# Changing the start of an attention and gated-MLP kernel: dummies, transpose order, one load's queue, and where one column block is accumulated

## The chip, the cores and the metric

The kernel runs on one core of a Trainium2 chip. The metric is the device time of one execution in microseconds. Where "slow execution" is said below, a difference of one or two us is meant. Most numbers of this document come from the profile of one execution per kernel. Its span (first to last instruction) is some 2 us shorter than the device time of the same execution.

## The reference, cut to what matters

```python
def reference(A_x, A_k_cache, A_v_cache, A_wq, A_wo, B_x, B_W_gate, B_W_up, B_W_down):
    xn = _layernorm(A_x)                     # A_x: 1 x 2048 x 512, bf16
    s = _A_ref(xn, A_k_cache, ...)           # attention, 32 heads of 128, 2048 keys, then @ wo
    gate = xn @ B_W_gate                     # 512 -> 1792
    up = xn @ B_W_up
    h = relu(gate) * up
    g = silu(h @ B_W_down)
    return A_x + s * g
```

The part at stake is the very start: load the first 512 rows of x, normalise, transpose, and begin the gate and up products of those rows.

## The kernel before: the parts that matter

TensorE (PE) needs the rows transposed. For the first 512 rows, the kernel only centres them on VectorE (DVE), transposes on PE into the two accumulator banks `ps_acc`, and copies to `xcT` on ScalarE (ACT). Four "tiles" of 128 rows are handled one by one, so that PE can begin early. The scale is put in later.

The first three column blocks of 128 columns ("head blocks" 0 to 2) are computed tile by tile, with 128-column matmuls. They hold the three double-bank slots of a ring in `ps_r`. Column block 3 and later ones use 512-column matmuls over all four tiles.

```python
warm_w = sem_ln1.sig(dve.memset(warm[:], 0.0))
load_x0(sp, 0)                        # 128 rows each
load_x0(act, 1)
load_w(sp, Wg_sb, wg_src, sem_wg, 0)  # gate columns 0..383
load_w(act, Wu_sb, wu_src, sem_wu, 0) # up columns 0..383
load_x0(sp, 2)
load_x0(act, 3)
...
def head_ln():
    ctok = {0: head_transpose(0, head_center(0))}
    warm_mm(2)
    for n in range(4):
        if n + 1 < 4:
            ntok = head_center(n + 1)
        _wait(pe, ctok[n])            # ScalarE's copy of tile n
        head_tile(n, 0)               # 4 gate + 4 up matmuls of 128 columns
        if n + 1 < 4:
            ctok[n + 1] = head_transpose(n + 1, ntok)
        for fc in range(1, HFC):      # HFC = 3
            head_tile(n, fc)
...
# emit_gate_up, for fc >= HFC:
s = ring_acquire()                    # waits until slot s has been read out
...
_wait(pe, warm_w)
warm_mm(10)                           # dummies: 128x512 matmuls on zeros
head_ln()
```

The dummies do no work. They keep PE busy while the first rows are on their way. The Trainium skill (the notes on the chip; "TensorE: Matmul & The Clock Gate", Part 1) says that the array starts at half its clock and is let up after a busy window of about 3.4 us; the windows run freely, whenever the kernel starts. Traces agree about the two rates: dummies start 427 ns apart at first and 216 ns apart later.

The softmax here doesn't subtract the row's maximum and nothing guards it: scores larger than these inputs give would overflow.

## Time and profile before

| | before |
|---|---|
| device time, median (range) of 5 executions | 1286.96 us (1286.37 to 1287.04) |
| span of the profiled execution | 1284.64 us |
| PE busy | 1278.8 us |
| first gate/up matmul | 6.214 us |
| column block 3 starts | 12.834 us |
| span minus start of block 3 | 1271.80 us |

The page's first part, of the kernel before, gives busy time, share of the span, and number of instructions by engine; its chain of waits gives shares of the span:

```profile
PE 1278.8 (100%) x12040; PEld 835.2 (65%) x12040; DVE 380.6 (30%) x685; ACT 1001.7 (78%) x1109; POOL 13.2 (1%) x25
...
PE 99%; DVE 1%; ACT 0%; issue 0%; DVEq 0%
```

PE is never long without work. Only holes in PE's stream, or PE at half clock, can be won back. The holes before 15 us stand in the timeline of that window. Columns: start and length in us, engine, line, operation, output<-inputs, shapes, count; in brackets the idle time before it and what ended it. Only lines that the argument uses are shown.

```profile
1.19 4.12 PE L374 MATMUL ps_r<-warm 128*128 128x512 bf16 x10 [1.19 <-DVE warm L239]
...
5.15 0.39 PE L364 MATMUL ps_acc<-ident,xc_sb 128*128 128x128 bf16 x4
...
5.57 0.58 ACT L369 COPY xcT<-ps_acc 128x512 bf16<-128x512 bf16 x1 [1.79 <-PE ps_acc L364]
5.63 0.35 DVE L354 TENSOR_SCALAR xc_sb<-x_sb,mv 128x512 bf16<-128x512 bf16 x1
6.21 0.40 PE L402 MATMUL ps_r<-xcT,Wg_sb 128*128 128x128 bf16 x4 [0.25 <-ACT xcT L369]
...
8.23 0.39 PE L364 MATMUL ps_acc<-ident,xc_sb 128*128 128x128 bf16 x4
...
8.66 0.59 ACT L369 COPY xcT<-ps_acc 128x512 bf16<-128x512 bf16 x1 [0.98 <-PE ps_acc L364]
...
9.35 0.39 PE L402 MATMUL ps_r<-xcT,Wg_sb 128*128 128x128 bf16 x4
...
11.34 1.57 ACT L454 ACTIVATE gr_sb<-ps_r 128x512 bf16<-128x512 f32 x3 [0.53 <-PE ps_r L402]
...
12.04 0.69 DVE L460 TENSOR_TENSOR hT<-gr_sb,ps_r 128x512 bf16<-128x512 bf16 x1 [2.93 <-PE ps_r L402]
...
12.83 1.02 PE L488 MATMUL ps_r<-xcT,Wg_sb 128*128 128x512 bf16 x4 [0.42 <-ACT gr_sb L454]
```

How to read it: a group of four 128-column matmuls shows 0.39 us, but the next group starts 0.22 us later. One matmul is recorded with 219 ns, of which only the first 56 ns keep the next one from starting. So a hole is measured from start to start, minus 56 ns (216 ns for 512 columns); the bracket shows less.

From 6.21 to 12.25 there is no hole at all. The transposes of tile 2 stand at 8.23, the copy runs 8.66 to 9.25, and tile 2 begins in its turn. Then comes the one hole of 0.58 us, from 12.25 to 12.83: column block 3 needs slot 0, which VectorE finishes reading at 12.73. The bracket blames ScalarE's relu, but the instruction that ended last before PE went on is the VectorE product at 12.04 to 12.73.

### The profile page before, as it was taken

The page shows a single profiled execution, that of the slowest core. Times are in us where ns is not written, and L with a number is a line of the kernel's source. Part 1 is how long each engine was busy: PE and PEld are TensorE (multiplying, and loading weights), DVE is VectorE, ACT ScalarE, POOL GpSimd, SP SyncE. Part 2 cuts the span into 40 slices and gives each one's busy share as a digit, 9 for nine tenths or more (in the row PEclk, how much of TensorE's full clock was granted, in tenths as well). Part 3 has the DMA queues.
Part 4 walks back from the last instruction along what each step waited for, and adds up shares of the span by engine and source line. Part 5 has one row for each costly group of instructions (what it writes and reads, how often), then busy time and mean ns, then how long its engine had stood idle before and what let it go on. Part 6 is the DMA issues. An engine that isn't in the chain of part 4 may idle for free.

```text
span 1284.6 us, 26946 instructions
## 1 busy us (share of the span) xinstructions
PE 1278.8 (100%) x12040; PEld 835.2 (65%) x12040; DVE 380.6 (30%) x685; ACT 1001.7 (78%) x1109; POOL 13.2 (1%) x25
## 2 busy tenths in 40 slices
PE   9999999999999999999999999999999999999998
PEld 5444476666666666666666666666666666666665
DVE  6433311112222222222222222222222222234455
ACT  3322399998888888888888888888888888888884
POOL 2100000000000000000000000000000000000000
PEclk9999999999999999999999999999999999999999
DMA  9600123232222332332321322323323312333202
GB/s 262 131 1 1 22 48 53 62 55 38 36 53 46 71 55 50 55 70 51 54 47 31 66 47 53 55 67 55 55 51 71 54 34 38 51 67 55 51 13 75
DMA packets 240977, 72.13 MB, mean 56 GB/s; under 512 B 227808, under 2 KB 240864, under 8 KB 240864
## 3 DMA queue, kind: packets, MB, share of 16 engines
q1 hardware_dynamic: 240048, 69.76, 28.5%
q8 instruction: 96, 1.57, 0.5%
q10 hardware_dynamic: 816, 0.66, 0.2%
q14 instruction: 17, 0.14, 0.0%
HBM read 32.77 MB, written 2.10 MB: 27 GB/s over the span
## 4 chain that ended last, share of the span: by engine, by line
PE 99%; DVE 1%; ACT 0%; issue 0%; DVEq 0%
PE ps_acc L742 36%; PE ps_r L645 34%; PE ps_r L578 9%; PE ps_r L599 8%; PE ps_acc L511 4%; PE ps_r L488 4%; PE ps_r L492 4%; PE ps_r L779 1%; DVE fin_tmp L787 0%; PE ps_r L402 0%; PE ps_r L374 0%; DVE x_sb L803 0%; ACT gr_sb L454 0%; PE ps_acc L364 0%; ACT xcT L369 0%
## 5 line engine op out<-in xcount | busy, mean ns | idle before, releaser
L655 ACT ACTIVATE PT<-ps_r 128x1024 bf16<-128x1024 f32 x1024 | 952.5, 1054 | 167.7 <-PE ps_r L645 167.7
L742 PEld LDWEIGHTS ps_acc<-V_sb,PT 128*128 128x128 bf16 x8192 | 620.9, 98 | 241.8 <-ACT PT L655 3.5
L742 PE MATMUL ps_acc<-V_sb,PT 128*128 128x129 bf16 x8192 | 776.9, 220 | 0.0
L645 PE MATMUL ps_r<-QT_sb,KT_sb 128*128 128x512 bf16 x2048 | 754.5, 379 | 0.0
L672 DVE RECIPROCAL rz_sb<-ps_acc 128x4 f32<-128x4 f32 x127 | 23.2, 183 | 729.8 <-PE ps_acc L742 729.8
L645 PEld LDWEIGHTS ps_r<-QT_sb,KT_sb 128*128 128x128 bf16 x2048 | 194.9, 98 | 1.1 <-DVE QT_sb L589 0.4
L578 PE MATMUL ps_r<-xnT,Wq_sb 128*128 128x512 bf16 x512 | 130.9, 379 | 0.0
L599 PE MATMUL ps_r<-Wo_sb,OT_store 128*128 128x512 bf16 x448 | 114.6, 379 | 0.0
L589 DVE CAST QT_sb<-ps_r 128x512 bf16<-128x512 f32 x128 | 88.5, 691 | 48.2 <-PE ps_r L578 48.2
L578 PEld LDWEIGHTS ps_r<-xnT,Wq_sb 128*128 128x128 bf16 x512 | 49.8, 97 | 60.7 <-ACT PT L655 27.1
L675 DVE TENSOR_TENSOR Onorm<-ps_acc,rz_sb 128x512 bf16<-128x512 f32 x127 | 87.8, 691 | 4.4
L599 PEld LDWEIGHTS ps_r<-Wo_sb,OT_store 128*128 128x128 bf16 x448 | 43.8, 98 | 52.9 <-ACT PT L655 0.2
L454 ACT ACTIVATE gr_sb<-ps_r 128x512 bf16<-128x512 f32 x56 | 32.9, 595 | 49.2 <-PE ps_r L488 48.7
L612 DVE TENSOR_TENSOR s_acc<-s_acc,ps_r 128x512 f32<-128x512 f32 x96 | 66.0, 687 | 17.4 <-PE ps_r L599 17.4
L460 DVE TENSOR_TENSOR hT<-gr_sb,ps_r 128x512 bf16<-128x512 bf16 x56 | 38.4, 685 | 46.9 <-PE ps_r L492 42.2
L511 PE MATMUL ps_acc<-Wd_sb,hT 128*128 128x512 bf16 x224 | 49.0, 379 | 0.0
L492 PE MATMUL ps_r<-xnT,Wu_sb 128*128 128x512 bf16 x168 | 43.1, 379 | 0.0
L488 PE MATMUL ps_r<-xnT,Wg_sb 128*128 128x512 bf16 x168 | 43.1, 379 | 0.0
L511 PEld LDWEIGHTS ps_acc<-Wd_sb,hT 128*128 128x128 bf16 x224 | 21.9, 98 | 26.5 <-DVE g_sb L528 0.3
L519 ACT ACTIVATE sig_sb<-ps_acc 128x512 f32<-128x512 f32 x12 | 7.2, 597 | 29.5 <-PE ps_acc L511 29.5
L492 PEld LDWEIGHTS ps_r<-xnT,Wu_sb 128*128 128x128 bf16 x168 | 16.4, 98 | 19.8
L488 PEld LDWEIGHTS ps_r<-xnT,Wg_sb 128*128 128x128 bf16 x168 | 16.4, 98 | 19.8
(50 smaller groups left out, 182.1 us busy)
## 6 DMA issues: line engine op xcount, KB each, us to landing
V_sb<-in_A_v_cache_dram SPq DMA_DIRECT2D x32, 512.0 KB, 4.6
Wq_sb<-in_A_wq_dram SPq DMA_DIRECT2D x32, 128.0 KB, 2.5
Wo_sb<-in_A_wo_dram SPq DMA_DIRECT2D x8, 512.0 KB, 4.9
OT_store<-Onorm SPq DMA_TRANSPOSE x127, 2.4
Wd_sb<-in_B_W_down_dram SPq DMA_DIRECT2D x1, 1792.0 KB, 14.6
x_sb<-in_A_x_dram SPq DMA_DIRECT2D x3, 512.0 KB, 12.1
out_dram<-x_sb SPq DMA_DIRECT2D x6, 256.0 KB, 2.2
Wg_sb<-in_B_W_gate_dram SPq DMA_DIRECT2D x1, 768.0 KB, 12.0
```

What stands on the lines that cost most here:

```text
L460: dve.tensor_tensor(hT[par][:, fc, :], gr_sb[gk][:], ps_r[:, gb + 1, :], ALU.mult)
L488: ins = pe.matmul(ps_r[:, gb, :], Wg_sb[:, c, fs], xT[:, c, xs], start=(c == 0), stop=(c == DC - 1))
L492: ins = pe.matmul(ps_r[:, gb + 1, :], Wu_sb[:, c, fs], xT[:, c, xs], start=(c == 0), stop=(c == DC - 1))
L511: ins = pe.matmul(ps_acc[:, jb, 0:D], hT[par][:, fc, j * 128:(j + 1) * 128], Wd_sb[:, fc, :], start=(fc == 0), stop=(fc == FC - 1))
L578: ins = pe.matmul(ps_r[:, bank, :], Wq_sb[b][:, c, :], xnT[:, c, qs], start=(c == 0), stop=(c == DC - 1))
L589: etok = sem_qpe.sig(dve.tensor_copy(QT_sb[b][:, qs], ps_r[:, bank, :]))
L599: ins = pe.matmul(ps_r[:, bank, 0:D], OT_store[g % 2][:, hh, n * 128:(n + 1) * 128], Wo_sb[g % 2][:, hh, :], start=(hh == 0), stop=(hh == ...
L612: dve.tensor_tensor(s_acc[:, n, :], s_acc[:, n, :], ps_r[:, bank, 0:D], ALU.add)
L645: ins = pe.matmul(ps_r[:, 2 * s + tt, :], KT_sb[h % 2][:, t * 128:(t + 1) * 128], QT_sb[h % 2][:, qs], start=True, stop=True)
L655: act.activation(PT[pb][:], ps_r[:, 2 * s:2 * s + 2, :], ACTF.Exp, scale=scale)
L675: dve.tensor_tensor(Onorm[ob][:], o_ap, rz_sb[:].to_broadcast([128, 4, Dh]), ALU.mult))
L742: ins = pe.matmul(o_ap, PT[pb][:, tt, j * 128:(j + 1) * 128], V_sb[vb][:, t, 0:VW], start=(t == 0 and j % 2 == 0), stop=(t == KT - 1 and j ...
```

## The change

Its intent, as its description has it: start the dummies sooner, from constants that exist already, and use fewer of them; put the second tile's transposes ahead of the first gate/up; load rows 256 to 511 through one queue; compute column block 3 in the accumulators, which are idle then, so that it need not wait for a slot.

```diff
-        warm = S_([128, D], BF16, "warm")
...
-                warm_w = sem_ln1.sig(dve.memset(warm[:], 0.0))
                 load_x0(sp, 0)
                 load_x0(act, 1)
                 load_w(sp, Wg_sb, wg_src, sem_wg, 0)
                 load_w(act, Wu_sb, wu_src, sem_wu, 0)
                 load_x0(sp, 2)
-                load_x0(act, 3)
+                load_x0(sp, 3)
...
+                ones_w = nc.const_aps.tensor(1.0, [128, 128], BF16)
+                ones_r = nc.const_aps.tensor(1.0, [128, NQ], BF16)
...
                 def head_ln():
-                    ctok = {0: head_transpose(0, head_center(0))}
-                    warm_mm(2)
+                    ctok = [head_transpose(0, head_center(0))]
+                    warm_mm(1)
+                    ctok.append(head_transpose(1, head_center(1)))
+                    ntok = {2: head_center(2), 3: head_center(3)}
                     for n in range(4):
-                        if n + 1 < 4:
-                            ntok = head_center(n + 1)
                         _wait(pe, ctok[n])
-                        head_tile(n, 0)
-                        if n + 1 < 4:
-                            ctok[n + 1] = head_transpose(n + 1, ntok)
-                        for fc in range(1, HFC):
+                        for fc in range(HFC):
                             head_tile(n, fc)
+                            if fc == 1 and n in (1, 2):
+                                ctok.append(head_transpose(n + 1, ntok[n + 1]))
...
+                def gu_banks(s):
+                    if s is None:
+                        return ps_acc[:, 0, :], ps_acc[:, 1, :]
+                    return ps_r[:, 2 * s, :], ps_r[:, 2 * s + 1, :]
...
-                        s = ring_acquire()
-                        gb = 2 * s
+                        if Q == 0 and fc == HFC:
+                            s = None
+                            _wait_all(pe, acc_free)
+                        else:
+                            s = ring_acquire()
+                        g_ps, u_ps = gu_banks(s)
...
-                _wait(pe, warm_w)
-                warm_mm(10)
+                warm_mm(8)
                 head_ln()
```

The transposes of tiles 2 and 3 stood behind head block 0 of the tile before; now they stand behind head block 1.

## The prediction

> **What bounds the kernel now.** TensorE: the page gives PE 1278.8 of 1284.6 us busy, and the chain of waits is 99% PE. The change touches only the first 15 us, so only PE idle or cold time there can be won. The timeline of that window shows:
>
> - 1.19 us: first dummy, after the VectorE memset of their operand (0.86 to 1.13). Dummies start every 427 ns until 4.58, then every 216 ns; the granted clock record begins at 4.85.
> - The four transposes of tile 0 wait for centred rows (VectorE ends 4.77), then stand behind the tenth dummy: 5.15. ScalarE's copy runs 5.57 to 6.16, the first gate/up starts 6.21.
> - From 6.21 to 12.25 PE streams without a hole: 24 groups of four 128-column matmuls and three groups of transposes, 0.223 us each. Tiles 1 to 3 begin just after their copies end (7.68, 9.25, 10.81): transposes, then two head blocks (0.89 us), nearly exactly cover the 0.39 us to the last transpose's end plus the 0.585 us copy.
> - 12.25 to 12.83: PE waits for ring slot 0 (relu 0 at 11.34, product 0 to 12.73), 0.58 us. After it, PE has no hole.
>
> **What the change does.**
>
> 1. Column block 3 in the accumulators: it need not wait for slot 0. Gain up to 0.58 us.
> 2. Tile 1's transposes before the first gate/up: one group of 0.223 us leaves the stream. But they need VectorE's second centring, which ends 5.98 whatever else moves. So transposes at about 6.08, first gate/up at about 6.30: 0.09 us later, though tile 0's copy is ready some 0.25 us sooner. Net gain 0.13.
> 3. Transposes of tiles 2 and 3 move from after head block 0 to after head block 1. Now only one head block (0.446 us) stands between them and the tile that needs the copy. From the first transpose to the next tile takes 0.387 + 0.036 + 0.585 + 0.052 = 1.06 us; PE has 0.223 + 0.446 = 0.67 us of work. Two new stalls of 0.39 us, loss 0.78.
> 4. Fewer dummies, from constants: they start near 0.78, eight end near 4.2, then PE is idle until 4.87. Not on the path itself. The Trainium skill ("TensorE: Matmul & The Clock Gate", Part 1) says the clock is released after a busy window of about 3.4 us that runs freely; here it came 3.66 us after the first dummy. Eight dummies are 3.42 us, so in some executions the window will not count as busy and head tiles run at half rate: an estimated 1 to 1.5 us lost, in perhaps a quarter of executions.
> 5. Rows 384 to 511 on the SyncE queue: x landings shift by tenths, VectorE is the limit. Zero.
>
> Sum with a warm clock: -0.58 - 0.13 + 0.78 = +0.07 us. With the clock's risk about +0.3.
>
> **Prediction:** 1287.2 us, 1286.0 to 1288.6 eight times in ten. Faster by over 2%: 0.00; within 2%: 1.00; slower: 0.00.
>
> **What would show it.** In the timeline of the first 15 us: no hole before column block 3, which starts near 12.9 instead of 12.83 (right: steps 1 to 3 cancel); two holes of about 0.4 us before tiles 2 and 3, ended by ScalarE's copy (step 3); transposes of tile 1 at about 6.08 ended by VectorE's centring (step 2); matmul starts 56 ns apart from 6.3 on (warm) or 107 ns (cold, step 4). Busy time after 15 us unchanged.
>
> **What would make it wrong.** The clock released late, or later than in before, in most executions: 1288 or more. Or the copies being quicker, or transposes placed earlier than the order on PE says: then up to 0.7 us faster. Or x landing late on the one queue, so that VectorE's third centring holds up PE.

## The result, and the profile after

| | before | after |
|---|---|---|
| device time, median (range) of 5 executions | 1286.96 (1286.37 to 1287.04) | 1287.20 (1286.33 to 1288.24) |
| span of the profiled execution | 1284.64 | 1284.98 |
| first gate/up matmul | 6.214 | 6.236 |
| column block 3 starts | 12.834 | 13.181 |
| span minus start of block 3 | 1271.80 | 1271.80 |

The ratio is 1.0005, with a 95% interval of 0.9991 to 1.0019: the same within noise. Ratios here are the mean time of one kernel's fast runs over that of the other's of the same rounds, so not quite the ratio of the medians quoted.

The first trap is on the page of the changed kernel:

```profile
PE 1266.7 (99%) x11810; PEld 834.8 (65%) x12037; DVE 380.4 (30%) x684; ACT 1001.6 (78%) x1109; POOL 13.3 (1%) x25
...
PE 85%; ACT 12%; issue 1%; DVE 1%; DMA 0%; ACTq 0%; DVEq 0%
```

PE has not lost 12 us of work, and ScalarE has not come onto the path. There are 11810 matmul records for 12037 weight loads, and the kernel has one load for each matmul. Records are missing, and the chain goes astray at the missing ones: in e9 below, the same kernel with all 12037 records, it is 99% PE again.

The timeline of the first 16 us of the changed kernel:

```profile
0.77 3.57 PE L374 MATMUL ps_r<-const-bfloat16-1.0 128*128 128x512 bf16 x8 [0.77 <-PEq L891]
...
4.88 0.43 PE L361 MATMUL ps_acc<-ident,xc_sb 128*128 128x128 bf16 x4 [0.54 <-DVE xc_sb L351]
...
5.36 0.59 ACT L366 COPY xcT<-ps_acc 128x512 bf16<-128x512 bf16 x1 [2.19 <-PE ps_acc L361]
...
5.59 0.35 DVE L351 TENSOR_SCALAR xc_sb<-x_sb,mv 128x512 bf16<-128x512 bf16 x1
6.00 0.40 PE L361 MATMUL ps_acc<-ident,xc_sb 128*128 128x128 bf16 x4 [0.47 <-DVE xc_sb L351]
6.24 0.39 PE L401 MATMUL ps_r<-xcT,Wg_sb 128*128 128x128 bf16 x4
...
6.78 0.40 PE L401 MATMUL ps_r<-xcT,Wu_sb 128*128 128x128 bf16 x4 [0.16 <-DMA Wu_sb<-in_B_W_up_dram]
...
8.80 0.39 PE L361 MATMUL ps_acc<-ident,xc_sb 128*128 128x128 bf16 x4
...
9.22 0.59 ACT L366 COPY xcT<-ps_acc 128x512 bf16<-128x512 bf16 x1 [2.20 <-PE ps_acc L361]
...
9.86 0.40 PE L401 MATMUL ps_r<-xcT,Wg_sb 128*128 128x128 bf16 x4 [0.23 <-ACT xcT L366]
...
11.83 0.40 PE L401 MATMUL ps_r<-xcT,Wg_sb 128*128 128x128 bf16 x4 [0.23 <-ACT xcT L366]
...
12.97 0.69 DVE L464 TENSOR_TENSOR hT<-gr_sb,ps_r 128x512 bf16<-128x512 bf16 x1 [3.79 <-PE ps_r L401]
13.40 0.81 PE L499 MATMUL ps_acc<-xcT,Wg_sb 128*128 128x512 bf16 x3
```

What to see:

- Two new holes, before tile 2 (9.469 to 9.863) and before tile 3 (11.437 to 11.831), each 0.394 us. Both end when ScalarE's copy is done.
- The old hole before block 3 is gone. The 13.40 is misleading: three of four gate matmuls are recorded, the first one is missing, and block 3 began one slot (216 ns) earlier, at 13.181. VectorE is still busy with head block 0 then, until 13.66; block 3 did not wait for it.
- A hole that nobody predicted: 6.459 to 6.779, 0.32 us, ended by the arrival of the first part of W_up, which landed at 6.733. In the profile before it landed at 6.244.
- From the first gate/up to block 3: 6.620 us before, less 0.580 for the slot wait, less 0.223 for one group of transposes, plus 2 times 0.394, plus 0.320 for W_up, makes 6.925. Measured: 6.945.

The executions tell something else too. Two of the five, 1288.20 and 1288.24, stand apart from 1286.33, 1286.79 and 1287.20.

### The profile page after: what moved, and what is told of

The parts are those of the page before. It is cut to its first block, busy times and chain, and to the rows that moved or that the text cites. A ratio compares the mean times of both kernels' runs of the same rounds, so it can differ in the third digit from the quotient of the medians.

```text
span 1285.0 us, 26711 instructions
## 1 busy us (share of the span) xinstructions
PE 1266.7 (99%) x11810; PEld 834.8 (65%) x12037; DVE 380.4 (30%) x684; ACT 1001.6 (78%) x1109; POOL 13.3 (1%) x25
## 3 DMA queue, kind: packets, MB, share of 16 engines
q8 instruction: 96, 1.57, 0.6%
## 4 chain that ended last, share of the span: by engine, by line
PE 85%; ACT 12%; issue 1%; DVE 1%; DMA 0%; ACTq 0%; DVEq 0%
PE ps_acc L752 32%; PE ps_r L655 25%; ACT PT L665 12%; PE ps_r L588 9%; PE ps_r L609 8%; PE ps_acc L522 4%; PE ps_r L499 3%; PE ps_r L503 3%; PE ps_r L789 1%; DMA Wu_sb<-in_B_W_up_dram 0%; DVE fin_tmp L797 0%; PE ps_r L401 0%; DVE x_sb L813 0%; ACT xcT L366 0%; PE ps_acc L503 0%
## 5 line engine op out<-in xcount | busy, mean ns | idle before, releaser
L655 PE MATMUL ps_r<-QT_sb,KT_sb 128*128 128x512 bf16 x1837 | 675.1, 379 | 0.3
```

What stands on the lines that cost most here:

```text
L655: ins = pe.matmul(ps_r[:, 2 * s + tt, :], KT_sb[h % 2][:, t * 128:(t + 1) * 128], QT_sb[h % 2][:, qs], start=True, stop=True)
```

## The experiments

Twelve runs were made, in three sets of four; each set shared its runs of the kernel before (nine executions, medians 1286.96, 1286.96 and 1286.95). Each set had another chip, but these medians agree to 0.01 us. All gave a correct result. Every run was profiled once, so the reading of each rests on one profile.

Theory A: placing tile 2's and tile 3's transposes later costs two holes of 0.39 us; the accumulators save 0.58; tile 1's early transposes save a little. Theory C: the load order made W_up land late; rival D: its landing wanders. Theory E: the slow executions come from a late release of the clock, because eight dummies do not always fill a window; rival F: they come from the landing of the weights.

This table is the summary. "Block 3" is where column block 3 starts, with a missing record put back where one is missing (for e4: the last head matmul plus its slot).

| run | first gate/up | block 3 | from one to the other | span | W_up lands |
|---|---|---|---|---|---|
| before | 6.214 | 12.834 | 6.620 | 1284.64 | 6.244 |
| after | 6.236 | 13.181 | 6.945 | 1284.98 | 6.733 |
| e1 transposes behind block 0 | 6.311 | 12.270 | 5.959 | 1284.24 | 6.443 |
| e2 rows 384 to 511 on ScalarE's queue | 6.265 | 12.882 | 6.617 | 1284.68 | 6.176 |
| e3 ten dummies | 6.458 | 13.074 | 6.616 | 1284.88 | 5.465 |
| e4 four dummies | 6.285 | 14.686 | 8.401 | 1286.49 | 6.843 |
| e5 e3 with block 3 in the ring | 6.328 | 13.538 | 7.210 | 1285.33 | 6.394 |
| e6 before with accumulators | 6.741 | 12.916 | 6.175 | 1284.71 | 7.053 |
| e7 before with tile 1 early | 5.981 | 12.752 | 6.771 | 1284.55 | 6.216 |
| e8 gains only | 6.401 | 12.208 | 5.807 | 1284.01 | 5.951 |
| e9 after, again | 6.289 | 12.904 | 6.615 | 1284.70 | 5.567 |
| e10 six dummies | 6.477 | 15.300 | 8.823 | 1287.10 | 6.130 |
| e11 e8 with eight dummies | 6.127 | 11.934 | 5.807 | 1284.18 | 6.067 |
| e12 e8, row queue as before | 6.250 | 12.056 | 5.806 | 1283.96 | 6.156 |

Span minus block 3 is 1271.80 or 1271.81 in all but e1 (1271.97), e11 (1272.24) and e12 (1271.91), of which more below.

### e1: transposes of tiles 2 and 3 back behind head block 0

```diff
-                            if fc == 1 and n in (1, 2):
+                            if fc == 0 and n in (1, 2):
```

> The changed kernel with one condition changed back: the transposes of tiles 2 and 3 stand after head block 0 instead of head block 1. Theory A (the placement makes two PE holes of 0.39 us): the holes before tiles 2 and 3 close to under 0.05 us each, column block 3 starts about 0.79 us earlier relative to the first gate/up matmul (5.4 to 5.7 us from it instead of 6.95), and the fastest execution is some 0.8 us faster than the changed kernel's. Rival B (ScalarE's copy is late for another reason, so the placement is not what costs): holes of 0.3 us or more remain.

Measured: 1286.11 us (1285.92 to 1286.37). The holes before tiles 2 and 3 are gone. The timeline of e1 around them:

```profile
7.75 0.35 DVE L351 TENSOR_SCALAR xc_sb<-x_sb,mv 128x512 bf16<-128x512 bf16 x1
7.87 0.39 PE L401 MATMUL ps_r<-xcT,Wu_sb 128*128 128x128 bf16 x4
...
8.25 0.38 PE L361 MATMUL ps_acc<-ident,xc_sb 128*128 128x128 bf16 x4
...
9.37 0.39 PE L401 MATMUL ps_r<-xcT,Wg_sb 128*128 128x128 bf16 x4
...
10.93 0.39 PE L401 MATMUL ps_r<-xcT,Wg_sb 128*128 128x128 bf16 x4
```

Tile 2 begins at 9.37 and tile 3 at 10.93, each in its turn. But block 3 comes 5.959 us after the first gate/up, not the 5.4 to 5.7 expected: that figure was set too low. 6.945 less 2 times 0.394 less the W_up hole of 0.320 would be 5.837. The rest is a small hole, 8.095 to 8.254, 0.16 us (the sum then comes 0.04 too high): tile 2's transposes now come so early that VectorE's centring (done at 8.106) is late. So the later placement has something to say for it, for tile 2 and by 0.16 us here, against two holes of 0.394. The fastest execution was 0.41 us faster than the changed kernel's (1285.92 against 1286.33), not the 0.8 expected. Theory A stands for where the holes come from, and rival B falls.

### e2: rows 384 to 511 back on ScalarE's queue

```diff
-                load_x0(sp, 3)
+                load_x0(act, 3)
```

> The changed kernel with rows 384 to 511 back on ScalarE's queue. Theory C (moving them to SyncE's queue made the first block of W_up land 0.5 us later, 6.73 against 6.24, and opened the unpredicted PE hole of 0.32 us inside the first head block): W_up lands at 6.2 to 6.3 and the hole is under 0.1 us. Rival D (the landing wanders by half a us from one execution to the next whatever the queue): no fixed relation; W_up may land at 6.5 or later here too.

Measured: 1288.46 us (1286.52 to 1289.02), with three of five executions at 1288.46 or above. W_up landed at 6.176 and the hole was gone, as theory C has it. One profile with the right sign is not proof, and in e3 W_up landed at 5.465 with the rows on SyncE's queue. The later profiles speak against C: W_up landed at 5.465 to 6.843 in nine profiles with the rows on SyncE's queue, 6.156 to 7.053 in five with them on ScalarE's (read from the table). In e6 and e7, which are the old kernel in this respect, it was 7.053 and 6.216. The same kernel, after and e9, had 6.733 and 5.567. The landing wanders by over a microsecond whatever the queue; rival D stands, and C is not needed. A small effect of the queue on top of the wander is not excluded by these few profiles.

The Trainium skill ("DMA: Bandwidth & Descriptors", Queues, rings and completion order) says that every DMA engine takes turns between the queues it has work for, packet by packet. The traces bear this out only in part. The first parts of W_gate and W_up come through two queues, and packets of both move in the same stretches, but not evenly: from 3.0 to 4.0 us ScalarE's queue, which carries W_up, moved 55 of 366 packets in the changed kernel's profile and 336 of 412 in e9's. The order of landing changed with it (W_gate 5.703 and W_up 6.733 in the changed kernel's profile, 6.126 and 5.567 in e9's). What sets the shares is not shown.

### e3 and e4: ten dummies, four dummies

```diff
-                warm_mm(8)
+                warm_mm(10)     # e3
+                warm_mm(4)      # e4
```

> The changed kernel with ten dummies first instead of eight, still from constants. Theory E (with eight, the dummies end at 4.2 us and in some executions the clock is released a window later, which makes the executions at 1288.2): no execution above 1287.4, spread under 1 us as in the kernel before (1286.37 to 1287.04). Rival F (the spread comes from the landing of the first weights, not the clock): executions about 1288 remain in one or two of five.

> The changed kernel with four dummies first instead of eight; they end near 2.5 us. Theory E: the clock is released late in most executions, matmul starts in the head tiles are 107 ns apart for some us after 6.3, and the median is 1 to 2 us above that of the changed kernel. Rival F (the clock does not depend on the dummies in this range): head tiles 56 ns apart and the median within 0.4 us of the changed kernel's.

Measured: e3 1286.67 us (1286.27 to 1287.27), no execution above 1287.4; the spread of 1.00 is just what was to be undercut. e4 1288.34 us (1287.64 to 1289.01). The timeline of e4 shows why:

```profile
6.29 0.63 PE L401 MATMUL ps_r<-xcT,Wg_sb 128*128 128x128 bf16 x4
...
7.29 0.63 PE L401 MATMUL ps_r<-xcT,Wg_sb 128*128 128x128 bf16 x4
7.72 0.63 PE L401 MATMUL ps_r<-xcT,Wu_sb 128*128 128x128 bf16 x4
...
9.85 0.39 PE L401 MATMUL ps_r<-xcT,Wg_sb 128*128 128x128 bf16 x4
10.08 0.39 PE L401 MATMUL ps_r<-xcT,Wu_sb 128*128 128x128 bf16 x4
```

Until 9.85 a group of four starts every 0.43 us, twice the 0.22 of later groups. The record of the granted clock begins at 9.850 in this profile, against 5.025 in the changed kernel's. The share that the windows view prints as the granted clock is no help here: it reads 1.00 in the stretch from 6 to 9 us too, though starts are at half rate; the record seems to begin only with the release. The start-to-start time is what tells.

Block 3 came 1.5 us later than in the changed kernel, with W_up about equally late in both (6.843 and 6.733). Theory E's other expectations were met, F's were not.

### e5: e3 with column block 3 in the ring again

```diff
-                        if Q == 0 and fc == HFC:
+                        if False:
                             s = None
```

> The kernel of e3 (changed kernel, ten dummies) with one more part undone: column block 3 goes to the ring of slots again instead of the accumulators. Theory A (the accumulators save the wait for slot 0 whatever stands before it): a hole of 0.55 to 0.6 us opens between tile 3 and column block 3, block 3 starts about 1.97 us after tile 3's first matmul instead of 1.35, and the median rises by about 0.58 us on e3's 1286.67, to 1287.25. Rival B (with the two new holes the slot would be free in time anyway, so that the accumulators save nothing here): no hole, and the median of e3 within 0.2 us.

Measured: 1287.42 us (1287.14 to 1287.88), 0.75 above e3's median. The timeline of e5 (one matmul record missing again, so block 3 starts at 13.538):

```profile
12.74 0.39 PE L401 MATMUL ps_r<-xcT,Wu_sb 128*128 128x128 bf16 x4
...
13.75 0.81 PE L499 MATMUL ps_r<-xcT,Wg_sb 128*128 128x512 bf16 x3 [0.63 <-ACT gr_sb L458]
```

The hole is 13.538 minus 12.960, 0.58 us. The accumulators save that even with the two new holes in front, because head block 0 of tile 3 and its read-out shift along with them.

### e6: the kernel before with the accumulators alone

```diff
+                def gu_banks(s):              # as in the change
...
-                        s = ring_acquire()
-                        gb = 2 * s
+                        if Q == 0 and fc == HFC:
+                            s = None
+                            _wait_all(pe, acc_free)
+                        else:
+                            s = ring_acquire()
+                        g_ps, u_ps = gu_banks(s)
```

> The kernel before with one part of the change alone: column block 3 in the accumulators. Theory A: the hole of 0.58 us before block 3 closes, block 3 starts 6.06 us after the first gate/up instead of 6.62, no hole opens in the next three blocks, median about 1286.4. Rival B (the wait comes back at column block 4, which now needs the slot): a hole of 0.2 us or more before block 4, and less than half of the gain. With rows 384 to 511 on ScalarE's queue, theory C has the first block of W_up land at 6.2 to 6.3; rival D anywhere between 5.4 and 6.9.

Measured: 1286.39 us (1285.94 to 1286.51), where 1286.4 was expected. The timeline of e6 (the first record of block 3 is missing here too, so it starts at 12.916, straight after head block 2):

```profile
12.69 0.39 PE L402 MATMUL ps_r<-xcT,Wu_sb 128*128 128x128 bf16 x4
...
13.13 0.81 PE L500 MATMUL ps_acc<-xcT,Wg_sb 128*128 128x512 bf16 x3
```

Block 3 came 6.175 us after the first gate/up; 6.06 was expected, and W_up, landing at 7.053, made a hole of 0.12. No hole opened in the blocks behind it (span minus block 3: 1271.80). So the wait did not come back later, and rival B falls.

Its profile shows one more cost of the old front: the clock came only at 6.207 here, all ten dummies ran at half rate and stood in front of tile 0's transposes, which started at 5.429, and the first gate/up came at 6.741. Dummies protect the clock, but they also delay what is behind them when it comes late.

### e7: the kernel before with tile 1's transposes early

```diff
-                    ctok = {0: head_transpose(0, head_center(0))}
+                    ctok = [head_transpose(0, head_center(0))]
                     warm_mm(2)
+                    ctok.append(head_transpose(1, head_center(1)))
+                    ntok = {2: head_center(2), 3: head_center(3)}
...
+                            if fc == 0 and n in (1, 2):
+                                ctok.append(head_transpose(n + 1, ntok[n + 1]))
```

> The kernel before with one part of the change alone: the transposes of tile 1 ahead of the first gate/up, those of tiles 2 and 3 left behind head block 0. Theory A: first gate/up 0.30 us after VectorE's second centring ends instead of 0.23, one group of 0.223 us out of the stream, so column block 3 starts 0.13 us earlier counted from that centring (6.72 us after it instead of 6.86); median within 0.3 us of before, which no 5 rounds will tell apart. Rival B (VectorE's third centring is then too late for tile 2's transposes, because they come 0.13 us earlier): a hole of 0.1 to 0.2 us there gives all of it back.

Measured: 1286.85 us (1286.36 to 1287.42). The first gate/up came 0.291 us after the second centring, as expected. But block 3 came 7.06 us after that centring instead of 6.72 (the first gate/up at 5.981 less 0.291 is its end, 5.690). The timeline of e7:

```profile
7.61 0.39 PE L401 MATMUL ps_r<-xcT,Wu_sb 128*128 128x128 bf16 x4
7.66 0.35 DVE L354 TENSOR_SCALAR xc_sb<-x_sb,mv 128x512 bf16<-128x512 bf16 x1
...
8.16 0.38 PE L364 MATMUL ps_acc<-ident,xc_sb 128*128 128x128 bf16 x4 [0.16 <-DVE xc_sb L354]
```

PE stood from 7.836 to 8.157, 0.32 us, for VectorE's third centring (7.66 to 8.01), which waits for rows 256 to 383; these landed at 6.690. Rival B was right in this profile, with a hole larger than the 0.1 to 0.2 it expected: on its own, this part of the change gained nothing. It pays only if those rows land early enough, or if the transposes of tile 2 come later (in e8, e11 and e12 they landed at 6.321 to 6.508, and there is no such hole).

### e8: the parts that gain, without those that lose

Against the changed kernel: tile 2's and 3's transposes behind head block 0, ten dummies, and for tile 0 the three gate blocks ahead of the three up blocks, so that W_up is needed later.

```diff
-                            head_tile(n, fc)
-                            if fc == 1 and n in (1, 2):
+                            if n > 0:
+                                head_tile(n, fc)
+                            if n == 0:
+                                head_tile(n, fc, (0,))          # gate only
+                            if n == 0 and fc == HFC - 1:
+                                for f2 in range(HFC):
+                                    head_tile(n, f2, (1,))      # up only
+                            if fc == 0 and n in (1, 2):
...
-                warm_mm(8)
+                warm_mm(10)
```

> All parts that theory A holds for gains, without those it holds for losses: the changed kernel with the transposes of tiles 2 and 3 behind head block 0, ten dummies, and tile 0's three gate blocks ahead of its three up blocks, so that the first W_up is needed 0.67 us after the first matmul instead of 0.22. Theory A: no hole over 0.2 us between the first gate/up and block 8; block 3 starts 6.0 to 6.2 us after the first gate/up; no execution at 1288; median 1285.8 to 1286.2, below every other kernel here. Rival: median not below e1's 1286.11 by more than 0.1, because the landing of the first weights or the third centring holds the stream instead.

Measured: 1285.83 us (1285.78 to 1286.28), ratio to before 0.9993, interval 0.9979 to 1.0007. Block 3 came 5.807 us after the first gate/up, less than the 6.0 to 6.2 expected, and there is no hole in between: 24 groups and two groups of transposes at 0.223 are 5.80. In this profile rows 256 to 383 landed early, at 6.321, so the third centring was in time. By the interval the gain over before is not clear of noise; by the profile it is 0.63 us (12.834 against 12.208).

### e9: the changed kernel once more

No edit.

> The changed kernel itself once more, eight dummies. Theory E (the clock is released a window late in some executions): one to three of five executions at 1287.9 or above, the others at 1286.3 to 1287.3, with few between; if the profiled one is a slow one, its granted clock record begins near 8 to 9.5 us and its head tiles run 107 ns apart. Rival F (a landing of the first weights that wanders makes the spread): a slow profiled execution shows the clock released before 6.5 us and the first W_gate or W_up landing over 1 us later than 6.2.

Measured: 1286.49 us (1286.42 to 1288.40), one execution of five slow. The profiled one was not. Its timeline gives the cleanest look at the change, since W_up landed early (5.567):

```profile
6.29 0.39 PE L401 MATMUL ps_r<-xcT,Wg_sb 128*128 128x128 bf16 x4
...
9.59 0.40 PE L401 MATMUL ps_r<-xcT,Wg_sb 128*128 128x128 bf16 x4 [0.23 <-ACT xcT L366]
...
11.55 0.40 PE L401 MATMUL ps_r<-xcT,Wg_sb 128*128 128x128 bf16 x4 [0.23 <-ACT xcT L366]
...
12.90 1.03 PE L499 MATMUL ps_acc<-xcT,Wg_sb 128*128 128x512 bf16 x4
```

Block 3 starts at 12.904 here, with all four records present: 0.07 us later than in the profile before.

### e10: six dummies

```diff
-                warm_mm(8)
+                warm_mm(6)
```

> The changed kernel with six dummies, between e4's four and the changed kernel's eight. Theory E with a threshold on how much of a window is busy: more late releases than with eight (5 of 15 so far in the three kernels that have eight) and not more than with four (5 of 5): three to five of five at 1287.6 or above. Rival F: as with eight.

Measured: 1287.87 us (1286.28 to 1288.92), four of five slow, one as fast as the changed kernel's fastest. The profiled one was slow, with W_up early enough at 6.130 that no hole stands between the first gate and the first up:

```profile
6.48 0.63 PE L401 MATMUL ps_r<-xcT,Wg_sb 128*128 128x128 bf16 x4
6.90 0.63 PE L401 MATMUL ps_r<-xcT,Wu_sb 128*128 128x128 bf16 x4
...
11.14 0.39 PE L401 MATMUL ps_r<-xcT,Wg_sb 128*128 128x128 bf16 x4
```

Half rate until 11.1 us and then full rate. This is a slow execution whose cause can be seen: the clock, not the weights. Block 3 came at 15.300, 2.1 us after the changed kernel's.

### e11: e8 with eight dummies

```diff
-                warm_mm(10)
+                warm_mm(8)
```

> The kernel of e8 with eight dummies instead of ten. Theory E: fast executions as e8's (1285.8 to 1286.3), but one or two of five above 1287. Rival (with no other holes the release comes early enough with eight): all five under 1286.5.

Measured: 1285.99 us (1285.77 to 1287.51); four of five from 1285.77 to 1286.10 and one at 1287.51.

### e12: e8 with rows 384 to 511 on ScalarE's queue

```diff
-                load_x0(sp, 3)
+                load_x0(act, 3)
```

> The kernel of e8 with rows 384 to 511 back on ScalarE's queue. Theory C is already weak (e6 had these rows on ScalarE's queue and W_up landed at 7.05). If the queue does not matter, median within 0.3 us of e8's 1285.83 and W_up landing anywhere between 5.4 and 7.1; if SyncE's queue delays W_up, this one is faster than e8 or at least never slower.

Measured: 1285.88 us (1285.77 to 1286.63), ratio to before 0.9993, interval 0.9981 to 1.0006. Against e8's 1285.83, the queue makes no difference.

### What the dummies do, over all runs

Call an execution slow that lies over 1.2 us above the fastest one of its kernel (for e4, all of whose executions are near 1288, above the changed kernel's fastest, 1286.33):

| dummies in front, from constants | kernels | slow executions |
|---|---|---|
| 4 | e4 | 5 of 5 |
| 6 | e10 | 4 of 5 |
| 8 | after, e9, e1, e2, e11 | 2, 1, 0, 3, 1: 7 of 25 |
| 10 | e3, e5, e8, e12 | 0 of 20 |

This orders with the number of dummies, and not with the place of the rows or the transposes. No slow execution of an eight-dummy kernel was profiled, so for those the clock is inferred from this table and from e4's and e10's profiles. The cut at 1.2 us is rough: the kernel before, with ten dummies that start 0.4 us later, has executions at 1287.52 and 1287.57 in one set, 1.3 above its fastest there. What e6's profile shows, dummies at half rate in front of the transposes, may be their cause; no profile of one of them was taken. The chips do not explain the table: in the three sets, eight dummies ran on two chips and had slow executions on both; ten ran on all three and had none.

The traces hold more on the clock. The record at full rate lasts 1279.998 us in eleven profiles and 1276.585 us in three. These differ by 3.413 us and are 375 and 374 times 3.4133, so the clock seems to be set once per window of 3.413 us. Count windows back from each release, and take PE as busy from the start of a matmul until the next one could start. Then the window that ended with the release was 77 to 100% busy in all 14 profiles, and every window before it at most 71%. Nearest to the line are e2, released at 5.676 us after a window with 2.64 us of work, and e10, not released at 4.270 and 7.683 us after windows with 2.43 and 2.41. Counted this way, a window needs somewhere between 71 and 77%. (The transposes have to be counted as work for this: without them, e2's window has 2.26 us, less than e10's.)

Eight dummies take 3.42 us, but the border between two windows can split them so that neither window has enough. As an estimate from these numbers, with e10's stream at half rate, dummies added or left out, and the border anywhere with equal chance: a late release, at 9.2 to 10.2 us, in 18 to 29% of executions with eight dummies, none with ten, all with four, 68 to 100% with six. The table has 28, 0, 100 and 80%. This speaks for theory E; it remains an inference for the slow executions that were not profiled.

### Where a still faster front gives time back

In e1, e11 and e12 the span is 0.11 to 0.44 us longer behind block 3. In e11, 0.16 of it is a wait before column block 8 (20.73 us), most likely for the ring slot that a VectorE product frees at 20.63. The rest is in the first down product, in the timeline of e11:

```profile
34.13 1.28 ACT L538 ACT_TABLE_LOAD   x1 [2.13 <-DVE r2h L448]
35.42 0.69 ACT L538 ACTIVATE sig_sb<-ps_acc,r2h 128x512 f32<-128x512 f32 x1
...
37.41 1.63 PEld L530 LDWEIGHTS ps_acc<-Wd_sb,hT 128*128 128x128 bf16 x9 [0.61 <-DVE g_sb L547]
```

The third row tile needs the accumulator of the first, which passes through a table load on ScalarE, the tanh, and two VectorE operations. In the profile before, the weight load at this place waited 0.27 us. So a further gain of the front would be partly given back here as long as that chain is not shortened. That was not tried.

## Why the prediction was right

The predicted 1287.2 us was the measured median, 1287.20. That match to the hundredth is luck: the executions spread over 1.9 us, and in means the five of each kernel differ by 0.59 us (1287.35 against 1286.76), twice the 0.3 of the prediction, because two of five were slow where it counted on a quarter. The terms of its sum can be checked one by one.

1. Accumulators, gain up to 0.58 us: right. Undone on its own it costs 0.58 (e5), done on its own it closes the hole (e6).
2. Tile 1's transposes early, net gain 0.13: right inside the changed kernel, where the first gate/up came 0.291 us after the centring and one group left the stream. It does not hold for this part alone: in e7 the third centring was then late, and a hole of 0.32 us took more than the gain. The prediction said VectorE's third centring might hold up PE, but only as a danger of late rows in general. It did not see that in the changed kernel the later transposes avoid this.
3. Later transposes, two holes of 0.39 us, loss 0.78: right to about a hundredth, twice 0.394 (after, e2, e3, e5, e9). But the loss against the other placement is less, since that one can have its own hole: 0.16 us in e1, none in e8, e11 and e12.
4. Fewer dummies, "in perhaps a quarter of executions" 1 to 1.5 us lost: right in frequency, 7 of 25, and in kind as far as the profiles of e4 and e10 and the windows counted above reach. The size was a little larger: the changed kernel's three slow executions (after and e9) average 1288.28 and its other seven 1286.71, a difference of 1.57 us. Those seven are about the mean of the five executions of the kernel before, 1286.76.
5. Row queue, zero: right on the time (e8 against e12).

What the prediction missed was the landing of the first part of W_up. Its sum has no term for it, as if it landed at 6.244 again, as in the one profile before. In the profiled execution after, W_up landed at 6.733 and cost 0.32 us, which made the profile's difference 0.35 instead of 0.07. It goes with the execution rather than with the change: in e9, the same kernel, it landed at 5.567, and the difference is 0.07.

So the answer to where the expected gain went: the accumulators' 0.58 and the transposes' 0.13 were given back by the two copies that PE now waits for (0.79), and some executions lose 1.6 us on top, by all signs to a clock that comes late.

## What to carry to other kernels

When work is moved in an in-order stream, count what is left between each producer and its consumer: here 0.67 us of PE work had to cover a 1.06 us trip through ScalarE, and one condition turned a gain of 0.7 us into nothing. Dummies that warm the array should run until the real work is there; two dummies saved cost 1.6 us in a quarter of executions. And when a change is worth tenths of a microsecond, compare the time between two marks in the stream over several profiles, because a single profile's load landing can be off by more than the effect.

## What the Trainium skill lacked or had wrong

- "TensorE: Matmul & The Clock Gate", Part 1, names the window of about 3.4 us but not how busy a window has to be. Here dummies of 1.7 us (four, 427 ns each) were never enough (0 of 5), 2.6 us in 1 of 5, 3.4 us in 18 of 25, and 4.3 us in 20 of 20, counted by execution times as in the table above. Counted by windows, 77% was enough (e2) and 71% was not (e10).
- The same page, Back-to-back issue gap, gives about 81 ns for 128 and 131 ns for 512 columns as sustained spacing of weight load and matmul pairs. Here such pairs ran 56 ns and 216 ns apart, which is what the page calls the gap of a single matmul.
- The same page, Part 4, gives some 275 to 390 ns for a transpose of 128 by 128 on PE. Here transposes in the stream were recorded with 219 ns each at full rate and started 56 ns apart, as the matmuls around them.
- No page that was looked at gives the spread of a load's landing. The first part of W_up, issued at about 1.2 us in all 14 profiles, landed between 5.465 and 7.053 us.
